# Rounding and widening steps moved from ScalarE to GpSimd, three more warming products and another place for the second layer's weights

## The chip, the core and the metric

The kernel is one program on one core of one Trainium2 chip. The core has five engines with instruction streams of their own: TensorE (PE in the profile; PEld is its loading of weights), VectorE (DVE), ScalarE (ACT), GpSimd (POOL) and SyncE (SP), which here issues all DMA transfers. An engine runs its instructions strictly in the order in which they stand, so one that waits holds up all that stand behind it. The metric is the device time of one execution in microseconds (us), lower is better. TensorE's clock has two levels, 1.2 and 2.4 GHz; the profile gives the granted one as a share of full speed (1.0 or 0.5).

## What is computed

```python
# attention: 4 x 8 heads, 576 positions, head dimension 64
scores = q @ k.T / 8
cum  = cumsum(max(s, 0))
bias = min(-(cum[i] - cum[j]), 0);  causal mask
attn = softmax(scores + bias) @ v
x = attn heads side by side                       # 4 x 576 x 512
# gated part
gate = sigmoid(causal 5-tap convolution of x)     # one filter per channel
x = ((gate * (x @ w_val)) @ w_out)
# mixing part
u = x + (U V along the positions) applied to x    # rank 32
out = u + max(u @ w_ch1, 0) @ w_ch2               # 512 -> 2048 -> 512
```

The weights come in as float64 (the program reads their 32-bit words), q, k, v and s as float32; the result is float32.

## The kernel before

**Products in split form.** Most matrix products are done with operands in the format float32r, each operand cut into a rounded part and a rest: `a = ah + al`, `b = bh + bl`, and `a b` is taken as `ah bh + al bh + ah bl`, so three products for one. Two helpers make the parts: `rnd(kind, o, i)` writes the rounded part, `rest(kind, o, i, hi)` what is left. The name `kind` is looked up in the table `PLAN`, which gives the engine that does the step and a priority (`ahead`; a larger one is put earlier).

**q and k.** Heads 0 to 7, 16 and 30 use q and k as they are. For each of the 22 others `load_raw` brings q and k (transposed, 128 x 576 together) into a tile `qk`, of which there are two; `prep_head` rounds it into `hi` (kind `qk_hi`, line 334), takes the rest into `Q2` (kind `qk_lo`, line 335), and five DMA transfers ("put") lay the halves into the tiles `Q1`, `K1`, `Q2`, `K2` that the score products read. The rows of the profile call these tiles `Q` and `K`.

**Widening.** The weights are float64. `widen` makes the two float32r parts from the words in steps: `wd_a` scales the upper words (line 374), `wd_lim` clamps (line 375, GpSimd), four steps on VectorE (`wd`) build the upper part in `scr` and the lower part in a second scratch tile, and three GpSimd steps write the parts (`wd_hi`, `wd_rest`, `wd_lo`). For the weights of the gate, the value and the mixing products and of the first two blocks of the hidden layer, raw words and scratch lie in pieces of `uT` that are not yet in use (20 runs of `widen`, one of them for the 5 taps, spread between the heads by `side_step`). For blocks 2 to 15 of the hidden layer, raw words come into `raw` tiles and scratch is `scr0` (two buffers) and `scr1` (one), two runs for each block (`widen_w`), 28 in all.

**Attention.** For each head the scores of five blocks of rows are made on TensorE (`sc`), VectorE adds the mask and finds the maximum (`P`), ScalarE takes the exponent (`P`), TensorE turns the result over (`pt`), ScalarE and VectorE copy it out (`PTA`, `PTB`), and for each pair of heads `av` is made from it. Then `norm_rows` and `norm` divide by the row sums (`rs`, `wrs`), do the five taps and the gate. The dense products of a finished batch (`d`) run between the heads of the next.

**Hidden layer.** Sixteen blocks `m` of 128 hidden columns in groups of 2, 2, 3, 4, 3 and 2; for each group all five token tiles `t` are gone through: `ch1` makes 12 products `d` from weights `w1h`, `w1l` and the tokens `u`, ScalarE takes the relu (`hh`), VectorE its rest (`hl`), and `ch2` makes 12 products `acc` from `w2h`, `w2l`. The weights of block `m` lie in place `m % 7` of a ring. Places 0 and 1 lie in the pool `w0`, places 2 and 3 in `wb`, places 4, 5 and 6 in `ml`. `w0` is there from the start; `wb` is opened once the value products of the last batch are recorded, in the memory next to `wa`, which holds `scr0`, `scr1`, `hh` and `hl`; `ml` is opened last, on the other side of the memory, where `wo`, `U4`, `V4` and the gated values of the gated part lie until its last product.

**Order.** The program is recorded as written and then put in order by a scheduler that plays it through with times of its own and takes, for each engine, the ready instruction of the highest priority. So a change of engine or priority moves other instructions too.

**Start.** `WARM` products of 128 x 512 in bf16 on a tile of zeros run before the first scores (line 249).

Of the kernel before, what the change touches and what calls it, by code (L numbers as in the profile page):

```python
# [12 lines left out]
F32R = mybir.dt.float32r  # L13
# [8 lines left out]

PLAN = {
    "pace": ("gpsimd", 0),
    "qk_hi": ("scalar", 6000),
    "qk_lo": ("gpsimd", 2000),
    "put": ("sync", 3000),
    "wd_rest": ("gpsimd", 100),
# [4 lines left out]
    "uh": ("gpsimd", -2000),  # L33
    "ul": ("gpsimd", -6000),
    "u4": ("vector", 0),
    "wd_a": ("scalar", 6000),
    "wd_lim": ("gpsimd", 0),
    "wd": ("vector", -2000),
    "wd_hi": ("gpsimd", -2000),
# [42 lines left out]
RING = 7  # L82
# [7 lines left out]
ORDER = "T0 T1 S0 T2 T3 S1 S2 S3 T4 S4 A0 A1"  # L90
NPD = 6
DT = {"exp": 0.51, "xh": 0.96, "xl": 0.25, "tap": 1.5, "taps": 0.9, "tanh": 1.83, "gv": 4.3, "nl": 3.6, "rows": 10.0, "prep": 1.51}
WARM = 10


@with_exitstack
def fused_kernel(ctx, tc, qT, kT, vP, s, wval, wout, convw, U, V, w1, w2, rows01, out):
    nc = tc.nc
    B, H, D, S = qT.shape
    P = 128  # L100
# [113 lines left out]
    w0 = ctx.enter_context(tc.tile_pool(name="w0", bufs=1, side="right", reuse_waits="tile"))  # L214
# [32 lines left out]
    idle = psV.tile([P, 1024], F32, tag="av", name="idle")[:, 0:512]  # L247
    for _ in range(WARM):
        nc.tensor.matmul(idle, warm[:, 0:P], warm, start=True, stop=True)
# [118 lines left out]
    def widen(raw, scr, hi=None, lo=None, whole=None):  # L368

        a, t = scr  # L370
        au, tu = a.bitcast(U32), t.bitcast(U32)
        shrink = 2.0 ** -112
        steps = [
            lambda: rnd("wd_a", a, raw[..., 1].bitcast(F32), shrink),
            lambda: Via("wd_lim").tensor_scalar(a, a, LIMIT * shrink, -LIMIT * shrink, op0=ALU.min, op1=ALU.max),
            lambda: Via("wd").tensor_scalar(au, au, 3, None, op0=ALU.logical_shift_left),
            lambda: Via("wd").scalar_tensor_tensor(
                au, raw[..., 1], 0x80000000, au, op0=ALU.bitwise_and, op1=ALU.bitwise_or,
            ),
            lambda: Via("wd").tensor_scalar(tu, au, 0xFF800000, None, op0=ALU.bitwise_and),  # L380
            lambda: Via("wd").scalar_tensor_tensor(t, raw[..., 0], 2.0 ** -52, t, op0=ALU.mult, op1=ALU.mult),
        ]
        if whole is not None:
            return steps + [lambda: Via("wd").tensor_add(whole, a, t)]
        return steps + [
            lambda: rnd("wd_hi", hi, a),
            lambda: rest("wd_rest", a, a, hi),
            lambda: Via("wd_lo").tensor_add(lo, a, t),
        ]
# [5 lines left out]
    def pairs(t):  # L395
        return t.bitcast(U32).rearrange("p (n two) -> p n two", two=2)
# [58 lines left out]
    w12 = {m: {x: w0.tile([P, 512], F32R, tag=f"{x}{m}", name=x) for x in ("w1h", "w1l", "w2h", "w2l")} for m in range(2)}  # L455
# [306 lines left out]
    for n in range(NH + 1):  # L762
# [15 lines left out]
        m = n - 1  # L778
# [54 lines left out]
    TW = 512  # L833
# [5 lines left out]
    def load_w(k):  # L839

        m = k // 2
        if m < NF:
            raws[k] = wb.tile([P, 2 * TW], F32, tag="raw", name="raw") if k % 2 else raw1
            nc.sync.dma_start(raws[k].bitcast(U32), words(w2)[m * P:(m + 1) * P, :] if k % 2 else words(w1)[m])

    def widen_w(m):
        pool = w0 if m % RING < 2 else wb if m % RING < 4 else ml
        d = w12[m] = {x: pool.tile([P, TW], F32R, tag=f"{x}{m % RING}", name=x) for x in ("w1h", "w1l", "w2h", "w2l")}

        def part(nm, k):  # L850
            scr = [wa.tile([P, TW], F32, tag=f"scr{k}", name=f"scr{k}", bufs=2 - k) for k in range(2)]
            steps = widen(pairs(raws.pop(k)), scr, hi=d[nm + "h"], lo=d[nm + "l"])

            return steps[:6] + [lambda: load_w(k + 2)] + steps[6:]
        return [
            lambda: part("w1", 2 * m), lambda: part("w2", 2 * m + 1),
            lambda: ready.add(m),
        ]
# [65 lines left out]
    def mlp(i):  # L924

        for _ in pieces(i):
            steps[0] += rate.get(i, 0.0)
            side_step(int(steps[0]))
            steps[0] -= int(steps[0])
            yield  # L930
        if i in due:
            side_work.append(lambda m=due[i]: widen_w(m))
# [23 lines left out]
    wb = ctx.enter_context(tc.tile_pool(name="wb", side="right", **reuse))  # L956
# [6 lines left out]
    ml = ctx.enter_context(tc.tile_pool(name="ml", side="left", **reuse))  # L963
# [50 lines left out]
```

## Time and profile before

| | |
|---|---|
| median of 3 runs | 768.6 us (765.54 to 772.45) |
| the profiled execution | 766.13 us |
| its span, first to last instruction | 764.1 us |
| mean granted clock of TensorE | 0.986 |
| busy: PE, DVE, ACT, POOL | 738.7, 462.1, 300.6, 291.8 us |

The rows further down are of the profiled execution. "Idle" in brackets behind an instruction is the time that its engine stood still before it, and the arrow names what ended that. The starts of matrix products are measured, their ends are modelled, so a PE that is "busy" need not be at its pace. In the view of the chain, the work that ended last is followed back from the end of the execution.

### The profile page before, as it was taken

What the parts mean: (1) busy time and instruction counts of PE and PEld (TensorE: products, weight loads), DVE (VectorE), ACT (ScalarE), POOL (GpSimd) and SP (SyncE); (2) the same over time, 40 slices, a digit from 0 to 9 for tenths busy, and PEclk for the clock granted to TensorE, in tenths of its full rate; (3) what the DMA queues carried; (4) which work ended last, traced back from release to release, by engine and by line L of the source; (5) the groups of instructions that cost most, each with busy time, mean ns of one, the idle gap of its engine ahead of it and who ended that gap; (6) DMA issues with size and microseconds to landing.
All of it is one profiled execution on the core that took longest, in us unless ns stands there. A gap on an engine that the chain in (4) does not pass through costs nothing.

```text
span 764.1 us, 12182 instructions
## 1 busy us (share of the span) xinstructions
PE 738.7 (97%) x4366; PEld 619.2 (81%) x4366; DVE 462.1 (60%) x1053; ACT 300.6 (39%) x788; POOL 291.8 (38%) x323
## 2 busy tenths in 40 slices
PE   8998999999999999999899999999999999999997
PEld 5666889788787998798788888888888888888886
DVE  6878886787558655766749996424582234223234
ACT  5778666875677677533212211111121011010110
POOL 2566566445423243557197765102540024000000
PEclk8989999999999999999999999999999999999999
DMA  4663554644455432021103221100120000000023
GB/s 117 192 182 107 138 128 118 167 126 131 117 125 146 114 97 53 19 82 57 55 1 111 84 97 47 50 0 28 57 84 0 1 28 0 1 1 1 0 111 138
DMA packets 27000, 59.39 MB, mean 78 GB/s; under 512 B 4648, under 2 KB 5288, under 8 KB 26940
## 3 DMA queue, kind: packets, MB, share of 16 engines
q1 hardware_dynamic: 26940, 58.61, 27.2%
q8 instruction: 35, 0.57, 0.3%
q14 instruction: 25, 0.20, 0.1%
HBM read 37.04 MB, written 5.31 MB: 55 GB/s over the span
## 4 chain that ended last, share of the span: by engine, by line
PE 80%; DVE 6%; DMA 5%; ACT 4%; issue 2%; SPq 1%; POOL 1%; ACTq 0%; DVEq 0%; POOLq 0%
PE d L132 37%; PE acc L132 26%; PE pt L132 7%; PE av L132 5%; PE sc L132 5%; DVE uT L132 2%; DMA uT<-in_w 1%; DVE av L614 1%; DMA qk<-in_kT 1%; ACT P L132 1%; DVE P L132 1%; DMA K<-Q 1%; SPq L132 1%; ACT PTA L132 0%; ACT uT L132 0%
## 5 line engine op out<-in xcount | busy, mean ns | idle before, releaser
L132 PE MATMUL d<-u,w1h 128*128 128x512 f32 (+1 forms) x640 | 184.2, 371 | 0.0
L132 DVE SCALAR_TENSOR_TENSOR hl<-d,hh 128x512 fp32r<-128x512 f32 (+1 forms) x80 | 50.7, 634 | 170.4 <-ACT hh L874 170.1
L874 ACT ACTIVATE hh<-d 128x512 fp32r<-128x512 f32 (+1 forms) x80 | 44.3, 555 | 275.2 <-PE acc L132 149.5
L132 PEld LDWEIGHTS d<-u,w1h 128*128 128x128 f32 x640 | 116.0, 188 | 22.2
L132 PE MATMUL d<-u,w1l 128*128 128x512 f32 (+1 forms) x320 | 118.6, 371 | 0.0
L132 PE MATMUL acc<-hl,w2h 128*128 128x512 f32 (+1 forms) x320 | 105.0, 371 | 0.0
L132 PE MATMUL acc<-hh,w2h 128*128 128x512 f32 (+1 forms) x320 | 104.4, 372 | 0.5 <-DVE uT L132 0.5
L132 PE MATMUL acc<-hh,w2l 128*128 128x512 f32 (+1 forms) x320 | 101.9, 371 | 0.0
L132 ACT ACTIVATE P<-P,nm 64x64 f32<-64x64 f32 (+4 forms) x160 | 89.2, 562 | 28.3 <-DVE nm L132 27.9
L132 PE MATMUL sc<-K,Q 68*128 68x288 f32 (+13 forms) x384 | 91.7, 353 | 7.0 <-ACT PTA L132 2.0
L132 PE MATMUL pt<-ident,P 128*128 128x128 f32 x480 | 77.6, 286 | 7.0 <-ACT P L132 3.9
L132 DVE CUSTOM_DVE_ANT_0 P<-sc,causal 64x64 f32<-64x64 f32 (+4 forms) x160 | 65.1, 420 | 31.8 <-PE sc L132 27.6
L132 DVE TENSOR_TENSOR uT<-acc,uT 128x512 f32<-128x512 f32 (+1 forms) x120 | 70.1, 628 | 22.4 <-PE acc L132 22.2
L132 PEld LDWEIGHTS sc<-K,Q 68*128 68x128 f32 (+2 forms) x384 | 64.1, 198 | 16.2 <-ACT PTA L132 2.4
L132 PEld LDWEIGHTS d<-u,w1l 128*128 128x128 f32 x320 | 60.2, 188 | 11.0
L132 PEld LDWEIGHTS acc<-hh,w2h 128*128 128x128 f32 x320 | 58.7, 188 | 12.1 <-issue 0.9
L132 PEld LDWEIGHTS pt<-ident,P 128*128 128x128 f32 x480 | 55.5, 145 | 16.0 <-ACT P L132 7.0
L132 PEld LDWEIGHTS acc<-hl,w2h 128*128 128x128 f32 x320 | 58.8, 188 | 11.2
L132 PEld LDWEIGHTS acc<-hh,w2l 128*128 128x128 f32 x320 | 58.6, 188 | 11.3
L614 DVE SCALAR_TENSOR_TENSOR av<-X,cw,av 128x576 f32<-128x576 f32 x64 | 52.1, 814 | 4.4 <-ACT av L132 4.1
L132 DVE SCALAR_TENSOR_TENSOR scr<-raw,scr 128x512 uint32<-128x512 uint32 (+1 forms) x56 | 52.4, 936 | 1.4
L132 DVE TENSOR_SCALAR scr<-scr 128x512 uint32<-128x512 uint32 x56 | 43.4, 775 | 11.7 <-POOL w1l L132 6.3
(124 smaller groups left out, 1264.6 us busy)
## 6 DMA issues: line engine op xcount, KB each, us to landing
raw<-in_w SPq DMA_DIRECT2D x28, 512.0 KB
K<-hi SPq DMA_DIRECT2D x44, 144.0 KB
Q<-hi SPq DMA_DIRECT2D x44, 144.0 KB
V<-in_vP SPq DMA_DIRECT2D x16, 320.0 KB
out<-uT SPq DMA_DIRECT2D x16, 256.0 KB
qk<-in_qT SPq DMA_DIRECT2D x22, 144.0 KB
qk<-in_kT SPq DMA_DIRECT2D x22, 144.0 KB
K<-Q SPq DMA_DIRECT2D x22, 144.0 KB
```

Source lines behind the costliest of these rows:

```text
L132: return f(*args, **kw)
L614: Via("tap").scalar_tensor_tensor(g, X[:, k:k + S], cw[:, p, k:k + 1], g, op0=ALU.mult, op1=ALU.add,)
L874: Via("hh").activation(h_, o, AF.Relu)
```

## The change

Four edits: the rounding of q and k (`qk_hi`) goes from ScalarE to GpSimd, with priority 2000 in place of 6000; the first widening step (`wd_a`) goes from ScalarE to GpSimd, with priority 0 in place of 6000; `WARM` goes from 10 to 13; and of the places 2 to 6 of the ring, `w2h` and `w2l` now lie in `wb` and `w1h` and `w1l` in `ml`. On GpSimd a rounding is one `tensor_scalar` (line 143).

```diff
 PLAN = {
...
-    "qk_hi": ("scalar", 6000),
+    "qk_hi": ("gpsimd", 2000),
...
-    "wd_a": ("scalar", 6000),
+    "wd_a": ("gpsimd", 0),
...
-WARM = 10
+WARM = 13
...
     def widen_w(m):
-        pool = w0 if m % RING < 2 else wb if m % RING < 4 else ml
-        d = w12[m] = {x: pool.tile([P, TW], F32R, tag=f"{x}{m % RING}", name=x) for x in ("w1h", "w1l", "w2h", "w2l")}
+
+        d = w12[m] = {
+            x: (w0 if m % RING < 2 else wb if x[1] == "2" else ml).tile([P, TW], F32R, tag=f"{x}{m % RING}", name=x)
+            for x in ("w1h", "w1l", "w2h", "w2l")
+        }
```

ScalarE around the rounding of head 14 (`hi`), in the attention of the second batch, before:

```order
L132 ACTIVATE PTB_1289<-pt_1314 128x3x128
L132 ACTIVATE av_1210<-X0_94,cw_86 128x576
L132 ACTIVATE gvh_1369<-d_1330 128x288
L132 ACTIVATE PTB_1289<-pt_1346 128x4x128
L132 ACTIVATE hi_1618<-qk_1452 128x576
L132 ACTIVATE PTA_1288<-pt_1363 128x3x128
L132 ACTIVATE P10_88,sums1_97<-P10_88,nm_1101 128x192
L132 ACTIVATE P20_89,sums1_97<-P20_89,nm_1101 128x320
L132 ACTIVATE uT_58<-uT_58 128x160
```

The same place of ScalarE after the change (the numbers of the tiles are 3 higher):

```order
L132 ACTIVATE PTB_1292<-pt_1317 128x3x128
L132 ACTIVATE av_1213<-X0_94,cw_86 128x576
L132 ACTIVATE PTB_1292<-pt_1349 128x4x128
L132 ACTIVATE PTA_1291<-pt_1366 128x3x128
L132 ACTIVATE gvh_1372<-d_1333 128x288
L132 ACTIVATE P10_88,sums1_97<-P10_88,nm_1104 128x192
L132 ACTIVATE P20_89,sums1_97<-P20_89,nm_1104 128x320
```

The rounding and the scaling of the raw words (`uT_58<-uT_58 128x160`) no longer stand between the copies out of PSUM and the exponents.

GpSimd at about the same place, before (`xh`, `xl`: parts of a finished pair; `woh`, `wol`: parts of the output weights; line 375 is `wd_lim`):

```order
L375 TENSOR_SCALAR uT_58<-uT_58 128x512
L132 TENSOR_SCALAR woh_66<-uT_58 128x512
L143 TENSOR_SCALAR xh0_1310<-X0_94 128x576
L132 TENSOR_TENSOR uT_58<-uT_58,woh_66 128x512
L132 TENSOR_TENSOR xl0_1311<-X0_94,xh0_1310 128x576
L132 TENSOR_TENSOR wol_67<-uT_58 128x512
L132 TENSOR_TENSOR Q2_1455<-qk_1280,hi_1457 128x576
L375 TENSOR_SCALAR uT_58<-uT_58 128x160
```

And after:

```order
L143 TENSOR_SCALAR uT_58<-uT_58 128x512
L375 TENSOR_SCALAR uT_58<-uT_58 128x512
L143 TENSOR_SCALAR xh0_1313<-X0_94 128x576
L132 TENSOR_TENSOR xl0_1314<-X0_94,xh0_1313 128x576
L132 TENSOR_SCALAR woh_66<-uT_58 128x512
L132 TENSOR_SCALAR hi_1621<-qk_1455 128x576
L132 TENSOR_TENSOR uT_58<-uT_58,woh_66 128x512
L132 TENSOR_TENSOR Q2_1458<-qk_1283,hi_1460 128x576
L132 TENSOR_TENSOR wol_67<-uT_58 128x512
L143 TENSOR_SCALAR uT_58<-uT_58 128x160
```

The scaling now stands straight ahead of the clamp, and the rounding of head 14 stands ahead of the rest of head 13 (`Q2_1458`) and of the output weights' parts.

GpSimd at the opening of the hidden layer, before (`u27` is the last part of token tile 2; 5039 to 5042 are the parts of block 2, 5123 of block 3; token tiles 3 and 4 come behind these rows):

```order
L132 TENSOR_TENSOR u27_4872<-uT_58,u26_4871 128x512
L132 TENSOR_TENSOR scr0_5043<-scr0_5043,w1h_5039 128x512
L375 TENSOR_SCALAR scr0_5076<-scr0_5076 128x512
L132 TENSOR_TENSOR w1l_5040<-scr0_5043,scr1_5044 128x512
L132 TENSOR_SCALAR w2h_5041<-scr0_5076 128x512
L375 TENSOR_SCALAR scr0_5127<-scr0_5127 128x512
L132 TENSOR_TENSOR scr0_5076<-scr0_5076,w2h_5041 128x512
L132 TENSOR_TENSOR w2l_5042<-scr0_5076,scr1_5077 128x512
L132 TENSOR_SCALAR w1h_5123<-scr0_5127 128x512
```

And after, where the parts of token tiles 3 and 4 (`u37`, `u47` are their last) stand ahead (5042 to 5045 are the parts of block 2, 5126 and 5127 of block 3):

```order
L132 TENSOR_TENSOR u37_4996<-uT_58,u36_4995 128x512
L132 TENSOR_TENSOR u47_5102<-uT_58,u46_5101 128x256
L132 TENSOR_TENSOR w1l_5043<-scr0_5046,scr1_5047 128x512
L143 TENSOR_SCALAR scr0_5130<-raw1_4430 128x512
L132 TENSOR_TENSOR scr0_5079<-scr0_5079,w2h_5044 128x512
L375 TENSOR_SCALAR scr0_5130<-scr0_5130 128x512
L132 TENSOR_TENSOR w2l_5045<-scr0_5079,scr1_5080 128x512
L143 TENSOR_SCALAR scr0_5169<-raw_5115 128x512
L132 TENSOR_SCALAR w1h_5126<-scr0_5130 128x512
L375 TENSOR_SCALAR scr0_5169<-scr0_5169 128x512
L132 TENSOR_TENSOR scr0_5130<-scr0_5130,w1h_5126 128x512
L132 TENSOR_TENSOR w1l_5127<-scr0_5130,scr1_5131 128x512
```

Blocks 2 and 3 are now made behind the tokens, in the turn that blocks 4 and 5 had before.

## Rows read from the trace of the kernel before

**Rows 1.** The page's first part: busy time, share of the span, instructions.

```profile
PE 738.7 (97%) x4366; PEld 619.2 (81%) x4366; DVE 462.1 (60%) x1053; ACT 300.6 (39%) x788; POOL 291.8 (38%) x323
```

**Rows 2.** Stretches: length, busy time and count of PE, PEld, DVE, ACT, POOL; clock, DMA.

```profile
8.10:14.90 6.80, 6.80 (x25) 4.92 (x24) 4.58 (x19) 4.79 (x16) 0.00 (x0) 0.50 0.52 125
35.40:45.60 10.20, 9.66 (x36) 6.42 (x35) 5.78 (x22) 7.46 (x23) 5.10 (x6) 0.50 0.61 169
...
76.40:324.00 247.60, 236.62 (x1831) 206.05 (x1828) 178.79 (x533) 171.13 (x497) 113.72 (x128) 1.00 0.45 114
...
383.00:764.00 381.00, 376.79 (x1816) 313.65 (x1814) 185.24 (x281) 55.22 (x97) 109.37 (x108) 1.00 0.12 42
```

**Rows 3.** The chain that ended last, in time order: start, length, what.

```profile
6.58 4.48 PE sc L132 x12
...
105.90 3.68 DMA qk<-in_kT
...
267.95 3.57 DMA qk<-in_kT
```

**Rows 4.** ScalarE in order of time: instructions that a load had held up.

```profile
109.69 0.68 ACT L132 ACTIVATE hi<-qk 128x576 fp32r<-128x576 f32 x1 [2.47 <-DMA qk<-in_kT]
...
159.34 0.44 ACT L132 ACTIVATE uT<-uT 128x256 f32<-128x256 f32 x1 [1.28 <-DMA uT<-in_w]
...
184.05 0.45 ACT L132 ACTIVATE uT<-uT 128x256 f32<-128x256 f32 x1 [0.82 <-DMA uT<-in_w]
...
193.12 0.43 ACT L132 ACTIVATE uT<-uT 128x256 f32<-128x256 f32 x1 [1.04 <-DMA uT<-in_w]
...
233.04 0.69 ACT L132 ACTIVATE hi<-qk 128x576 fp32r<-128x576 f32 x1 [0.36 <-DMA qk<-in_kT]
...
271.71 0.69 ACT L132 ACTIVATE hi<-qk 128x576 fp32r<-128x576 f32 x1 [1.48 <-DMA qk<-in_kT]
```

**Rows 5.** Fourteen stretches in which ScalarE stood so, summed: length, then busy.

```profile
sum 27.86, PE 25.82 PEld 21.13 DVE 17.30 ACT 9.47 POOL 14.30; mean PE 1.84 PEld 1.51 DVE 1.24 ACT 0.68 POOL 1.02
```

**Rows 6.** Waits up to 330 us: who waited for whom, us, times, longest.

```profile
POOL uT L375 <- ACT uT L132: 33.1, 15, 14.0
...
ACT hi L132 <- DMA qk<-in_kT: 14.4, 12, 2.5
...
ACT uT L132 <- DMA uT<-in_w: 4.0, 4, 1.3
```

**Rows 7.** Groups by shape up to 330 us: count, busy and mean, idle before.

```profile
L132 ACT ACTIVATE hi<-qk 128x576 fp32r<-128x576 f32 x22 | 15.1, 685 | 18.3 <-DMA qk<-in_kT 14.4 <-DMA uT<-in_U 1.3 <-DMA K<-hi 0.9
...
L132 ACT ACTIVATE uT<-uT 128x512 f32<-128x512 f32 x8 | 5.4, 672 | 1.4 <-POOL wol L132 0.6 <-POOL wvl L132 0.6
```

**Rows 8.** One tile's instructions: count, shortest, median, longest ns, first and last start.

```profile
L132 DVE TENSOR_SCALAR scr<-scr x56: 408/468/1524, 333.9 to 646.8; 128x512 uint32<-128x512 uint32 x56
```

**Rows 9.** TensorE at the start, in order of time.

```profile
1.52 3.87 PE L249 MATMUL idle<-causal 128*128 128x512 bf16 x10 [1.52 <-DVE causal L245]
```

**Rows 10.** The chain in the hidden layer: runs of products.

```profile
434.60 5.69 PE acc L132 x25
...
493.11 8.40 PE acc L132 x36
```

**Rows 11.** GpSimd at the opening of the hidden layer, in order of time.

```profile
381.38 2.11 POOL L132 TENSOR_SCALAR u<-uT 128x512 fp32r<-128x512 f32 x4 [13.81 <-DVE uT L713]
383.45 0.64 POOL L132 TENSOR_SCALAR w1h<-scr 128x512 fp32r<-128x512 f32 x1
...
395.57 1.33 POOL L132 TENSOR_TENSOR w1l<-scr,scr 128x512 fp32r<-128x512 f32 x1
...
406.94 1.36 POOL L132 TENSOR_TENSOR w1l<-scr,scr 128x512 fp32r<-128x512 f32 x1
```

**Rows 12.** TensorE where blocks 2 and 3 begin, in order of time.

```profile
401.56 0.62 PE L132 MATMUL d<-u,w1h 128*128 128x512 f32 x2
...
409.32 0.62 PE L132 MATMUL d<-u,w1h 128*128 128x512 f32 x2
```

## The prediction

> **What bounds the kernel now.** I read the busy times first. PE is at 97% [rows 1], but its ends are modelled, so that figure can't tell work from waiting; the stretches by count can. In the hidden layer, from 383 us on, PE gets through 1816 products in 381 us, nearly all of 512 columns, with no idle time to speak of, while ScalarE is busy 55 us and GpSimd 109 us of it [rows 2]. There only a shorter product or a PE that starves would change the time. In the attention, from 76 to 324 us, no engine is full: DVE 179, ACT 171, POOL 114 of 248 us, and PE's 237 is stretched by products that wait for their inputs [rows 2]. That stretch is a mesh of short waits between four engines that each run in order, and a gain or a loss must come from there or from the start.
>
> Third, the chain of waits, since it says which waits reach the end. Between 100 and 275 us it passes six times through a transfer whose receiver is a ScalarE instruction that the change moves: the first and the last are shown, 3.68 us for q and k of head 14 and 3.57 us for head 31 [rows 3]. ScalarE in order of time then shows how long it stood still at those six: 2.47, 1.28, 0.82, 1.04, 0.36 and 1.48 us [rows 4], each time with a copy out of PSUM or an exponent queued behind.
>
> **What the change does to ScalarE.** It takes 22 roundings of 685 ns, 15.1 us, out of the attention, and the scalings of the raw words: 8 of 672 ns, 5.4 us, and 12 smaller ones that I count as 5 us [rows 7]. So about 25 us of work leave ScalarE there, of 171, and with them the stalls: 14.4 us at the roundings and 4.0 us at the scalings [rows 6]. Of that only what the chain needed counts. The six stalls sum to 2.47 + 1.28 + 0.82 + 1.04 + 0.36 + 1.48 = 7.45 us. I take **7.5 us saved**. The low end comes from fourteen such stretches taken together, 27.86 us long, in which PE was busy 25.82 [rows 5]: PE stood idle only 2.04 us there. The high end is the chain's whole share, six transfers of some 3.6 us, 21 us; I stay near the stalls, because most of each transfer had run before ScalarE reached its place. The 28 scalings in the hidden layer I count at nothing: ScalarE is busy 55 of 381 us there [rows 2], and behind PE's queue nothing waits for it.
>
> **What it does to GpSimd.** The same 25 us of work arrive there, since both engines need about 0.7 us for such a tile; busy time in the attention goes from 114 to about 138 of 248 us, 46 to 56%. Part of it falls into waits that vanish: GpSimd stood 33.1 us before the clamps for ScalarE's scaling, of which 14.0 us were one wait at the start [rows 6], and now it does the scaling itself. What is queued behind a rounding or scaling that waits for its load is the next clamp, the parts `xh` and `xl`, the rest `Q2` and, once per pair, the spreading of the row sums `wrs`. Only `wrs` leads straight to a product. With 10% more of the time taken, 16 times `wrs` meet a 0.7 us instruction in one case of ten and wait half of it, 0.6 us in all; and the stalls of 14.4 + 4.0 us, moved here, are met in 18.4 / 248 = 7% of the cases with about 1 us, 1.2 us in all. **1.8 us lost**, between 0 and the case of the second rival. The rest of a head often stands behind the next head's rounding now, as the order shows; the rest is wanted only a head later, so I count nothing for it, and the same rival is its bound.
>
> **Contention.** VectorE's widening step `scr<-scr`, from SBUF to SBUF, takes 408 ns at best, 468 at the median and 1524 at worst [rows 8]; over the 56 of them, the 19 with no GpSimd instruction beside them have a mean of 418 ns, the 11 with one beside them all the time 1340 ns. In the attention 40 such steps run, of 512 columns or fewer; with GpSimd busy 10% more of the time they lose 40 x 0.1 x (1.5 - 0.4) = 4.4 us of VectorE time at most. VectorE is busy 72% there and its share of the chain is small, so I take **0.6 us lost**, between 0 and 4.4. In the hidden layer VectorE has slack. The Trainium skill (GPSIMD Engine Reference, 1. Specifications) says that GpSimd's SBUF interface is shared with VectorE and contends with VectorE instructions in a two-port mode or with two SBUF inputs, which speaks against putting more on GpSimd. By that rule, taken at the high end, the sum would be 3.8 us worse; the spread of that one instruction agrees with the rule, and the exponents' and maxima's steps that read PSUM are not touched by it.
>
> **Thirteen warming products.** Ten run from 1.52 to 5.39 us [rows 9]; three more, 0.39 us each by the mean of the ten, end by 6.56 us, and the first scores begin at 6.58 [rows 3], so they fit into PE's idle gap and cost nothing. What they can give: behind that gap the clock stood at 0.5, 1.2 GHz, from 8.10 to 14.90 [rows 2]. The scores from 6.58 last 4.48 us, 3 us of them at the low level; at 2.4 GHz these take half, 1.5 us less. Behind them the chain goes over transfers for head 2. I take **0.7 us saved**, the middle of 0 and 1.5.
>
> **The place of the second layer's weights.** The products `acc` of blocks 2 and 3, whose weights lie in `wb`, run 25 in 5.69 us, 228 ns each; those of blocks 4 to 6, from `ml`, 36 in 8.40 us, 233 ns [rows 10]. The change puts the weights of blocks 4, 5, 6, 11, 12 and 13 into `wb`: 6 x 48 full products x 5.7 ns = 1.6 us. In return `w1` of blocks 2, 3, 9 and 10 leaves `wb`; if that costs the same per product for half of the tokens, 4 x 24 x 5.7 ns = 0.5 us. **1.1 us saved**, between 0 and 1.6.
>
> **Blocks 2 and 3.** Their `w1` now lies where the gated part's operands are read until its end, so it can be written no earlier than token tiles 3 and 4, at 381.4 us. Blocks 4 and 5 had that turn before: `w1l` done at 396.9 and 408.3 us [rows 11]. PE wants block 2 at 401.56 and block 3 at 409.32 [rows 12]. So they have a slack of 4.7 and 1.0 us; the added scaling of 0.7 us on GpSimd is made good by its no longer waiting for ScalarE. **Nothing lost**, but up to 5 us if GpSimd slips by one run of `widen` (396.9 to 408.3 is two).
>
> **The sum.** -7.5 + 1.8 + 0.6 - 0.7 - 1.1 = -6.9 us. The profiled execution took 766.13 us, 2 us outside its span, and lies 2.5 us under the median of 768.6; a change in microseconds carries over, so the median becomes 761.7. **Forecast 761.5 us**, 0.9% under before.
>
> **Rivals.** *The stalls were cover for others.* VectorE is busier than ScalarE in the attention (179 to 171 us), and PE was idle only 2.04 us in the fourteen stretches [rows 2, 5]; then the gain is 2.0, less 2.4 lost, with 1.8 from start and place: 767 us. For it speaks that small idle time; against it, that the chain ran through six of them.
>
> *GpSimd becomes the engine that is late.* The place is the pair's end: `wrs` behind a rounding that waits for its load. If each of the 16 pairs meets one stall of 14.4 / 12 = 1.2 us, that is 19 us, and the time 761.5 + 19 - 1.8 = 779 us, slower than before. It decides from 0.5 us per pair on, where 16 x 0.5 eats the gain. For it: GpSimd's order now has roundings and scalings between all its other steps; against: it had 46% load and long waits of its own.
>
> *Blocks 2 and 3 come late*: 761.5 + 5 = 766.5 us; for it speak the 1.0 us of slack and VectorE's four steps between GpSimd's, against it that ScalarE no longer stands in that row.
>
> *The clock.* From 35.4 to 45.6 us it was at 1.2 GHz [rows 2]. If PE, better fed, keeps 2.4 GHz there, half of the 9.66 us of PE time goes: 756.7 us; a new drop of that length elsewhere would cost as much.
>
> *The change doesn't do what it says*: the order shows roundings and scalings on GpSimd, so this is left to the clock at the start, which is in the range.
>
> **How the numbers follow.** Forecast and its neighbourhood (757 to 765) 0.38; a gain above it, by clock or by the high end of the stalls, 0.22; stalls as cover or late blocks, 765 to 771, 0.25; GpSimd late 0.15. A change of 1% (7.7 us) is about what a measurement of this kernel can tell from none; the bound lies at 760.9, inside the forecast's neighbourhood, so 0.20 of its 0.38 is beyond it. Faster by over 1%: 0.22 + 0.20 = 0.42; within 1%: the other 0.18 and the 0.25 of 765 to 771, 0.43; slower by over 1%: 0.15, as GpSimd late mostly means over 776. The range, 749 to 773, leaves out the far end of both sides.
>
> **What will show it.** No ScalarE wait on the loads of q, k or weights; GpSimd with such waits instead, and `wrs` waiting no longer than now. The chain in the attention with fewer transfers. `acc` of blocks 4 to 6 at 228 ns. PE without a wait at blocks 2 and 3. Clock at 1.0 behind 8 us. I would be wrong if PE's waits for `wrs` or for the rests grow, or if the new order lets PE fall idle where it did not.

## The result

The changed kernel took 759.64 us (median of 4 runs, 757.32 to 760.29) beside 767.22 us for the kernel before: a ratio of 0.9898, 95% interval 0.9859 to 0.9938. In a second comparison, with the experiments, it took 756.09 us (4 runs, 754.84 to 756.33) against 765.68 us (18 runs): 0.9865, 0.9839 to 0.9890. The forecast was 761.5 us, 0.9% under before. So the sum came out nearly right; what it was made of came out only in part.

The busy times of the changed kernel answer to [rows 1]. ScalarE lost 36 us, GpSimd gained 46, VectorE 11, and TensorE's (PE's) busy time fell by 5.5 us.

```profile
PE 733.2 (97%) x4369; PEld 617.8 (82%) x4369; DVE 473.0 (62%) x1053; ACT 264.5 (35%) x718; POOL 337.8 (45%) x393
```

The same view as [rows 2], stretches of the changed kernel:

```profile
8.10:14.90 6.80, 6.39 (x40) 4.56 (x39) 4.73 (x19) 5.43 (x19) 0.00 (x0) 1.00 0.54 129
35.40:45.60 10.20, 7.96 (x50) 4.82 (x49) 7.52 (x21) 4.67 (x15) 8.38 (x10) 0.83 0.67 185
76.40:324.00 247.60, 237.43 (x1821) 209.54 (x1820) 184.68 (x534) 157.69 (x462) 134.19 (x160) 0.99 0.45 112
383.00:757.00 374.00, 371.10 (x1796) 310.30 (x1794) 201.28 (x293) 41.25 (x75) 140.39 (x142) 1.00 0.14 48
```

Behind 8 us the granted clock is 1.0 and PE does 40 products where it did 25; between 35 and 46 us it does 50 instead of 36. But from 76 to 324 us, where the forecast's 7.5 us should have come from, PE does no more products in the same time than before (1821 against 1831). That stretch holds low stretches of the clock that come and go; further down it is read without them.

The first two instruction groups of TensorE, the start that answers to [rows 9]: thirteen warming products take 5.73 us, and the first scores begin at 7.04 us, not 6.58. They are quicker, though: 12 take 3.13 us here and took 4.48 us before [rows 3].

```profile
1.52 5.73 PE L249 MATMUL idle<-causal 128*128 128x512 bf16 x13 [1.52 <-DVE causal L245]
7.04 3.13 PE L132 MATMUL sc<-K,Q 66*128 66x64 f32 x12
```

Waits up to 330 us, the view of [rows 6]: what waited, for whom, us in total, times, longest.

```profile
POOL hi L132 <- DMA qk<-in_kT: 22.0, 11, 8.0
POOL wrs L132 <- DVE rs L132: 15.8, 9, 4.4
POOL uT L143 <- DMA uT<-in_w: 9.2, 6, 2.6
PE pt L132 <- POOL wrs L132: 3.9, 2, 2.1
```

ScalarE no longer waits for a load of q and k or of weights; GpSimd waits longer in its place than ScalarE did (22.0 against 14.4 us, 9.2 against 4.0). PE hardly notices. Two roundings on GpSimd in order of time, the second behind the longest of its waits for q and k:

```profile
254.01 0.68 POOL L132 TENSOR_SCALAR hi<-qk 128x576 fp32r<-128x576 f32 x1 [1.57 <-DMA qk<-in_kT]
...
268.00 0.68 POOL L132 TENSOR_SCALAR hi<-qk 128x576 fp32r<-128x576 f32 x1 [7.97 <-DMA qk<-in_kT]
```

PE's longest wait between 258 and 276 us is 0.03 us. From 20 to 100 us the chain goes over GpSimd at two places, both times over `wrs`. GpSimd's steps before 41 us in order of time, and the products that waited for the last of them:

```profile
38.52 1.27 POOL L132 TENSOR_TENSOR wvl<-uT 128x512 fp32r<-128x512 f32 x1
39.88 0.64 POOL L143 TENSOR_SCALAR uT<-uT 128x512 f32<-128x512 f32 x1
40.48 0.72 POOL L132 TENSOR_SCALAR wrs<-rs 128x640 f32<-128x640 f32 x1
```

```profile
41.26 1.16 PE L132 MATMUL pt<-ident,wrs 128*128 128x128 f32 x5 [2.10 <-POOL wrs L132]
```

A moved scaling (line 143) stands right before `wrs`, and PE stood 2.10 us. The scaling itself is 0.64 us of that, and it had waited for no load. The other wait, 1.82 us at 74 us, stands behind a step that was on GpSimd before too (the rest of the output weights, 1.27 us). So this is near the second rival's mechanism, without the load that it named; PE met it twice, 3.9 us in all, not 16 times.

Contention on VectorE is larger than I took it. One group by shape over the whole span, before and then after: the mean of the same 16 widening steps went from 337 to 600 ns.

```profile
L132 DVE TENSOR_SCALAR uT<-uT 128x256 uint32<-128x256 uint32 x16 | 5.4, 337 | 1.7 <-POOL uT L375 1.6
```

```profile
L132 DVE TENSOR_SCALAR uT<-uT 128x256 uint32<-128x256 uint32 x16 | 9.6, 600 | 3.5 <-POOL uT L375 3.3
```

The mean hides that few steps are hit, and these fully: before, one of the 16 took 1137 ns; after, four took 1414 to 1501 and one 528, and the others stayed at 230 to 300 ns. One of the four and the GpSimd step beside it:

```profile
165.97 1.50 DVE L132 TENSOR_SCALAR uT<-uT 128x256 uint32<-128x256 uint32 x1
```

```profile
165.89 1.43 POOL L132 TENSOR_TENSOR xl<-X,xh 128x576 fp32r<-128x576 f32 x1
```

VectorE's step starts 0.08 us behind GpSimd's and ends 0.15 us after it. The other three, and the one before the change, also start during a GpSimd step of 1.4 us with two operands and end 0.14 to 0.15 us after it.

In the hidden layer, the run of products `acc` that [rows 10] shows at 8.40 us, on the chain of the changed kernel:

```profile
488.49 8.17 PE acc L132 x36
```

8.17 / 36 = 227 ns, 233 before. And blocks 2 and 3, GpSimd's last step on `w1` and PE's first product, answering to [rows 11, 12]:

```profile
390.40 1.29 POOL L132 TENSOR_TENSOR w1l<-scr,scr 128x512 fp32r<-128x512 f32 x1
...
401.99 1.36 POOL L132 TENSOR_TENSOR w1l<-scr,scr 128x512 fp32r<-128x512 f32 x1
```

```profile
396.98 0.63 PE L132 MATMUL d<-u,w1h 128*128 128x512 f32 x2
...
404.79 0.63 PE L132 MATMUL d<-u,w1h 128*128 128x512 f32 x2
```

The slack is 396.98 - 391.69 = 5.3 us and 404.79 - 403.35 = 1.4 us; PE did not wait.

### The profile page after: what moved, and what is told of

It reads as the page before. It is cut to its first block, busy times and chain, and to the rows that moved or that the text cites. A ratio compares the mean times of both kernels' runs of the same rounds, so it can differ in the third digit from the quotient of the medians.

```text
span 757.3 us, 12161 instructions
## 1 busy us (share of the span) xinstructions
PE 733.2 (97%) x4369; PEld 617.8 (82%) x4369; DVE 473.0 (62%) x1053; ACT 264.5 (35%) x718; POOL 337.8 (45%) x393
## 3 DMA queue, kind: packets, MB, share of 16 engines
q1 hardware_dynamic: 26940, 58.61, 27.8%
## 4 chain that ended last, share of the span: by engine, by line
PE 85%; DVE 8%; issue 2%; DMA 2%; ACT 2%; POOL 1%; ACTq 0%; DVEq 0%; POOLq 0%
PE d L132 39%; PE acc L132 26%; PE pt L132 8%; PE av L132 6%; PE sc L132 5%; DVE P L132 2%; DVE uT L132 2%; DVE av L614 2%; DMA uT<-in_w 1%; ACT P L132 0%; DMA K<-Q 0%; DVE nl L132 0%; POOL uT L143 0%; DVE uT L313 0%; ACT PTB L132 0%
## 5 line engine op out<-in xcount | busy, mean ns | idle before, releaser
L877 ACT ACTIVATE hh<-d 128x512 fp32r<-128x512 f32 (+1 forms) x80 | 44.3, 556 | 342.8 <-PE acc L132 173.8
L132 ACT ACTIVATE P<-P,nm 128x576 f32<-128x576 f32 (+4 forms) x160 | 89.1, 560 | 36.9 <-DVE nm L132 36.3
L132 PE MATMUL sc<-K,Q 68*128 68x288 f32 (+13 forms) x384 | 87.8, 343 | 2.3 <-ACT PTA L139 1.5
L132 PE MATMUL pt<-ident,P 128*128 128x128 f32 x480 | 75.6, 282 | 5.0 <-ACT P L132 3.0
L132 PEld LDWEIGHTS acc<-hh,w2h 128*128 128x128 f32 x320 | 58.8, 188 | 11.5 <-issue 0.6
L132 PEld LDWEIGHTS acc<-hl,w2h 128*128 128x128 f32 x320 | 58.9, 188 | 10.9 <-DVE hl L132 0.3
L132 DVE SCALAR_TENSOR_TENSOR scr<-raw,scr 128x512 uint32<-128x512 uint32 (+1 forms) x56 | 55.7, 995 | 1.4
```

The costliest lines, as they stand in the source:

```text
L132: return f(*args, **kw)
L877: Via("hh").activation(h_, o, AF.Relu)
```

## The experiments

Twelve kernels in three groups of four, each group beside the kernel before on one chip. The groups ran on three chips, so across groups only ratios are compared. In short, q is the rounding of q and k on GpSimd, w the first widening step there, n thirteen warming products, p the place of the second layer's weights.

**Each edit alone.**

```diff
-WARM = 10
+WARM = 13
```

> The kernel before with thirteen warming products in place of ten, nothing else. By the forecast's own terms 0.7 us less, a ratio of 0.999. By the rival that came out of the trace of the changed kernel, the start: there the clock stood at 1.0 from 8.10 to 14.90 us and the 1.2 GHz stretch of 35.4 to 45.6 us was 3.4 us long instead of 10.2, and the stretch of 76 to 324 us was no shorter; then most of the gain is the clock's, and this kernel gains about 5 us, a ratio near 0.9935, with the granted clock at 1.0 behind 8 us.

Ratio 1.0013 (0.9986 to 1.0040). The stretch behind 8 us shows the clock up as in the changed kernel, and 38 products instead of 25:

```profile
8.10:14.90 6.80, 5.86 (x38) 4.10 (x37) 4.94 (x19) 5.22 (x19) 0.00 (x0) 1.00 0.52 126
```

Yet nothing is left of it at the end. The theory that the start alone makes the gain falls.

```diff
-    "qk_hi": ("scalar", 6000),
+    "qk_hi": ("gpsimd", 2000),
```

> The kernel before with the rounding of q and k on GpSimd, nothing else. By the forecast's terms it takes three of the six stalls away, 2.47 + 0.36 + 1.48 = 4.3 us, and brings some 1.3 us of GpSimd and contention cost: about 3.0 us less, a ratio of 0.996. By the start theory nothing (0.999 to 1.001), since the waits come back on VectorE and GpSimd; clock at 0.5 behind 8 us as before.

0.9966 (0.9940 to 0.9992), 2.6 us: the forecast's term. But in this kernel ScalarE's wait for raw words rose from 4.0 us to

```profile
ACT uT L132 <- DMA uT<-in_w: 10.1, 6, 3.0
```

```diff
-    "wd_a": ("scalar", 6000),
+    "wd_a": ("gpsimd", 0),
```

> The kernel before with the first widening step on GpSimd, nothing else. By the forecast's terms three stalls go, 1.28 + 0.82 + 1.04 = 3.1 us, against some 1.1 us of cost: about 2.0 us less, a ratio of 0.997. By the start theory nothing (0.999 to 1.001). If GpSimd becomes late, slower: the spreading of the row sums then waits longer than before.

1.0010 (0.9977 to 1.0042): nothing where 2.0 us were expected. ScalarE still waits for q and k, and once for v:

```profile
ACT hi L132 <- DMA qk<-in_kT: 13.8, 9, 2.2
...
ACT hi L132 <- DMA V<-in_vP: 7.7, 1, 7.7
```

```diff
-        pool = w0 if m % RING < 2 else wb if m % RING < 4 else ml
...
+            x: (w0 if m % RING < 2 else wb if x[1] == "2" else ml).tile([P, TW], F32R, tag=f"{x}{m % RING}", name=x)
...
```

> The kernel before with the second-layer weights of places 2 to 6 beside the relu's tiles, nothing else. Both theories: 1.1 us less, a ratio of 0.9986, with the products acc of blocks 4 to 6 at 228 ns in place of 233 and the first half of blocks 2, 3, 9 and 10 at 233 in place of 228. If the later turn of blocks 2 and 3 costs, PE waits at 401 or 409 us and the gain is gone.

0.9969 (0.9943 to 0.9995). The trace shows 1.1 us of it where it was expected: from the first product `acc` to the last, 400.3 us against 401.4 before, and the same run of 36 products on the chain:

```profile
495.44 8.17 PE acc L132 x36
```

The rest of the 2.4 us isn't explained by the edit: in its profiled execution this kernel was no faster than before up to the hidden layer.

**One edit left out.** The four ratios alone add up to 0.9958, so either the first figure was lucky or the edits help each other.

> The changed kernel once more, for a closer figure beside the three that follow. The four edits alone gave 1.0013, 0.9966, 1.0010 and 0.9969, which add up to 0.9958. Theory S, each edit by itself: this comes out near 0.994, the high end of its first interval. Theory I, roundings and scalings only help together, because a load that holds ScalarE up through the one takes its toll through the other (with the roundings alone away, its waits for raw words rose from 4.0 to 10.1 us): this stays near 0.990.

0.9865 (0.9839 to 0.9890), so they help each other: the sum 0.9958 is good to some 0.0056 (the root of the four half intervals squared and added; somewhat more, as the four share the runs of the kernel before), and 0.9865 lies 0.0093 from it. With the first comparison's 0.9898 taken in, weighted by the intervals, the changed kernel is at 0.9875, and what follows for single edits is 0.1% less.

> The changed kernel with the first widening step back on ScalarE. Theory S: leaving out an edit that gave nothing alone changes nothing, the ratio is that of the changed kernel. Theory I: ScalarE waits some 10 us for raw words again and loses most of the pair's gain, 4 us above the changed kernel, 0.995.

0.9939 (0.9916 to 0.9961): w, worth nothing alone, is worth 0.7% on top of the others.

> The changed kernel with ten warming products. Theories S and I: the ratio of the changed kernel, within 0.1%, since thirteen alone gave nothing. If the three products help only where the rest of the start is quicker, the clock stands at 0.5 from 8 to 15 us in all its executions and it is 2 to 5 us above the changed kernel, 0.993 to 0.996.

0.9957 (0.9931 to 0.9982): n, worth nothing alone, is worth 0.9%. Theories S and I both miss here; the rider about the three products holds. The profiled execution, 758.6 us, is the second fastest of twelve (758.4 to 767.2), so its trace doesn't show where these 7 us lie.

> The changed kernel with the second-layer weights where they were. Both theories: 1.1 to 2.4 us above the changed kernel, 0.0015 to 0.003 in the ratio, with the products acc of blocks 4 to 6 at 233 ns.

0.9891 (0.9864 to 0.9918): p is worth 0.26%, about what it gave alone, but good only to some 0.4%. Without it the 36 products on the chain are back at 233 ns:

```profile
484.21 8.40 PE acc L132 x36
```

**The pair, the last edit left out, and spare products against the clock.**

> The kernel before with both ScalarE edits, the roundings of q and k and the first widening step on GpSimd, nothing else. The forecast's terms: 7.5 us saved, 1.8 + 0.6 us lost, 5.1 us less, a ratio of 0.9933. Theory S: the two alone add up, 0.9966 + 0.0010, 0.9976. Theory C, the clock decides: without the three warming products the 1.2 GHz stretch behind 8 us stays, and it comes out with the kernel that lacked only those products, less the place's 0.0015: 0.997, with a mean clock near 0.990.

0.9943 (0.9921 to 0.9965), 4.4 us where the forecast's terms gave 5.1. So the pair's size was right. It is more than the two alone add up to (0.9976), but that sum is itself good only to 0.004, so the difference isn't clear of the noise.

> The changed kernel with the rounding of q and k back on ScalarE. Theory S: 0.34% above the changed kernel, 0.990. Theory I, that both kinds of step have to leave ScalarE: ScalarE waits some 10 us and more for q and k, and most of the gain is gone, 0.996 or above. Theory C: its ratio goes with its clock, about 0.35 us for each 0.001 of the mean clock that it lacks against the changed kernel.

0.9995 (0.9975 to 1.0014): without q nothing of the change is left. On top of the other three q is worth 1.3%, alone it gave 0.34%. Theory S falls. Theory I's ratio holds, but not its reason: ScalarE's wait for q and k was 7.7 us here, not over 10.

The last two kernels issue spare products in more heads:

```diff
     def fill(ps, n):
-        if phase[0] <= 2:
+        if phase[0] <= 7:
```

> The kernel before with the two spare products ahead of each transposition, which its first three heads have, issued for heads 3 to 7 as well: some 36 pairs of 0.23 us, 8.3 us of TensorE work that no result needs, between 31 and 80 us. Theory C: the 1.2 GHz stretches of 35 to 45 us and 73 to 76 us vanish, the mean clock rises by some 0.008, up to 6.8 us are regained against what of the 8.3 us is not in idle gaps; the time falls or stays, 0.994 to 1.000. Without the clock's part (the order alone made the change quicker): 2 to 8 us slower, 1.003 to 1.010.

1.0080 (1.0056 to 1.0104), slower. The spare products, one group by shape from 28 to 85 us (35 pairs), took their time:

```profile
L132 PE MATMUL pt<-causal 128*128 128x256 bf16 x70 | 13.2, 281 | 0.5 <-ACT PTA L139 0.4 <-DVE wrs L132 0.2
```

but the mean clock of the runs stayed at 0.987 (before: 0.986). The low stretch moved, to where PE was again short of work:

```profile
47.00:50.40 3.40, 1.59 (x8) 0.99 (x9) 2.69 (x3) 2.79 (x9) 2.42 (x3) 0.68 0.25 57
74.40:81.20 6.80, 4.74 (x20) 3.97 (x19) 6.37 (x21) 5.88 (x16) 2.10 (x4) 0.59 0.43 124
```

So this run doesn't hold the clock up, and what the clock costs by itself can't be read from it.

> The changed kernel with the same spare products for heads 3 to 7. Theory C: its clock is near 1.0 already, so it gains at most one stretch of 3.4 us, 1.7 us, and pays the same work: 0 to 5 us above the changed kernel, and its distance to the kernel before with spare products is smaller than 9.6 us, about 5. If the order alone made the change quicker, the distance stays near 9.6 us.

0.9893 (0.9872 to 0.9915): 2.1 us above the changed kernel (good to some 2.6), as theory C allowed, but the distance to the filled kernel before grew to 14.2 us. Theory C, in the form that an evened-out clock shrinks the distance to 5 us, isn't borne out; nor is the other, that it stays near 9.6.

**Where in the program.** One place can be found in every trace: the first product `av<-PTB,V` of a pair of heads. Here are such rows, TensorE in order of time (narrow windows cut their runs short): for the kernel before the ones of the first, fourth, tenth, fourteenth and sixteenth pair; for the changed one of the first, fourth and sixteenth; for q alone of the same five; and for the changed one in the second comparison of the fourth, tenth and fourteenth.

```profile
27.25 0.55 PE L132 MATMUL av<-PTB,V 128*64 128x192 f32 x4
...
76.73 0.49 PE L132 MATMUL av<-PTB,V 128*64 128x192 f32 x4
...
206.84 0.55 PE L132 MATMUL av<-PTB,V 128*64 128x192 f32 x4
...
286.04 0.55 PE L132 MATMUL av<-PTB,V 128*64 128x192 f32 x4
...
321.62 0.55 PE L132 MATMUL av<-PTB,V 128*64 128x192 f32 x4
```

```profile
25.77 0.55 PE L132 MATMUL av<-PTB,V 128*64 128x192 f32 x4
...
70.38 0.50 PE L132 MATMUL av<-PTB,V 128*64 128x192 f32 x4
...
316.94 0.55 PE L132 MATMUL av<-PTB,V 128*64 128x192 f32 x4
```

```profile
28.58 0.54 PE L132 MATMUL av<-PTB,V 128*64 128x192 f32 x3
...
72.92 0.50 PE L132 MATMUL av<-PTB,V 128*64 128x192 f32 x4
...
207.12 0.55 PE L132 MATMUL av<-PTB,V 128*64 128x192 f32 x4
...
285.01 0.55 PE L132 MATMUL av<-PTB,V 128*64 128x192 f32 x4
...
320.61 0.38 PE L132 MATMUL av<-PTB,V 128*64 128x192 f32 x2
```

```profile
69.78 0.50 PE L132 MATMUL av<-PTB,V 128*64 128x192 f32 x4
...
198.85 0.55 PE L132 MATMUL av<-PTB,V 128*64 128x192 f32 x4
...
276.68 0.55 PE L132 MATMUL av<-PTB,V 128*64 128x192 f32 x4
```

The differences of such rows, and the time at 1.2 GHz in two of the stretches (added up from the granted clock in windows of about 1.7 us), in us; the fourth column is shown once more in parts:

| kernel | to the first pair | first to fourth | of it at 1.2 GHz | fourth to sixteenth | fourth to tenth | of it at 1.2 GHz | tenth to fourteenth | `acc`, first to last |
|---|---|---|---|---|---|---|---|---|
| before | 27.2 | 49.5 | 14 | 244.9 | 130.1 | 0 | 79.2 | 401.4 |
| p | 27.2 | 49.8 | 17 | 246.9 | 131.2 | 0 | 80.1 | 400.3 |
| n | 26.1 | 49.1 | 11 | 247.8 | 132.7 | 2 | 79.5 | 401.4 |
| w | 27.9 | 50.7 | 19 | 252.2 | 136.9 | 8 | 79.8 | 401.5 |
| n, p, w | 26.0 | 51.3 | 17 | 247.1 | 132.2 | 10 | 79.4 | 400.4 |
| q | 28.6 | 44.3 | 7 | 247.7 | 134.2 | 0 | 77.9 | 401.4 |
| q, n, p | 26.5 | 44.1 | 7 | 248.1 | 134.6 | 0 | 77.8 | 400.4 |
| q, w | 32.0 | 41.7 | 0 | 244.9 | 131.1 | 0 | 78.2 | 401.5 |
| q, w, p | 27.8 | 44.3 | 3 | 242.9 | 129.2 | 7 | 78.1 | 401.1 |
| q, w, n | 26.0 | 42.3 | 0 | 244.3 | 129.5 | 0 | 77.8 | 401.4 |
| all | 25.8 | 44.6 | 3 | 246.6 | 133.2 | 7 | 77.8 | 400.4 |
| all, again | 25.9 | 43.9 | 3 | 244.0 | 129.1 | 0 | 77.8 | 400.4 |

Most columns show one edit. The first falls to about 26 us with n. The second is 49 to 51 us without q and 42 to 45 with it, in every kernel. The fourth is 243 to 247 us with q and w together, 247 to 252 with one of them, 245 to 248 with neither. The last falls by 1 us with p (by 0.3 in q, w, p). Two cautions: the kernel before and p run the same attention and differ by 2 us in the fourth column; and each row is one execution, that of w the slowest of its twelve runs, that of q, w, p the second fastest.

The fourth column mixes in low stretches of the clock; its parts can be read without them. From the fourth to the tenth pair, seven traces have none: the kernel before and p take 130.1 and 131.2 us, the two kernels with q and without w 134.2 and 134.6, the three with both 129.1 to 131.1. So there q alone costs 3 to 4 us, and w takes that back. ScalarE's waits for raw words show how: 4.0 us before, 10.1 with q alone, none with w, and in q, n, p

```profile
ACT uT L132 <- DMA uT<-in_w: 12.9, 6, 3.9
```

The difference between q, n, p and the changed kernel there, 5.5 us, is about what w was worth on top of the others. From the tenth to the fourteenth pair no trace has a low stretch: 79.2 to 80.1 us without q, 77.8 to 78.2 with it, in every kernel.

**The clock.** In q and w together, PE was late between 18 and 29 us, and lost at the start what it won later:

```profile
18.30:28.50 10.20, 8.70 (x30) 5.97 (x32) 6.66 (x27) 6.19 (x19) 4.14 (x7) 0.55 0.53 176
```

The low stretches also change from one execution of a program to the next. Two stretches of the changed kernel, in the first comparison and in the second; the second line of each starts some 12 us behind the first `av<-PTB,V` of the fifteenth pair:

```profile
75.60:79.00 3.40, 3.40 (x17) 3.34 (x16) 2.07 (x9) 2.59 (x8) 1.72 (x3) 0.50 0.71 230
312.40:315.80 3.40, 3.34 (x28) 2.81 (x29) 1.75 (x7) 1.31 (x4) 2.81 (x4) 1.00 0.00 0
```

```profile
75.60:79.00 3.40, 3.40 (x28) 3.37 (x27) 3.36 (x12) 3.33 (x11) 2.59 (x3) 1.00 0.68 176
307.80:311.20 3.40, 3.40 (x17) 2.25 (x18) 0.75 (x3) 1.00 (x3) 2.11 (x3) 0.50 0.00 0
```

From the fifteenth to the sixteenth pair the ten traces of the table without a low stretch there take 16.7 us, and the two with one, of 3.4 us (q, w, n, and all, again), 18.1 and 18.2. So in that place a low stretch cost 1.5 us, 0.44 of its length. Taken at that price (an estimate), the low stretches make up most of the second column's difference: its mean is 50.1 us without q and 43.6 with it, and 43.2 and 42.1 with 0.44 of the low time taken off.

Over the 179 runs of the second comparison and the experiments, each kernel taken against its own level, a run whose mean clock is 0.010 lower takes 3.4 us longer. 0.010 of some 765 us is 15 us at the low level, which would cost 7.6 us if PE were at work all that time; by this slope it costs less than half of that, as it would if PE waited in much of it anyway. The changed kernel's mean clock was 0.998 in the second comparison and that of the kernel before 0.985; 0.013 of clock would be some 4.4 of the 9.6 us by this slope. From kernel to kernel the slope is twice that: over the ten without added spare products the ratios fall by 6.6 us for each 0.010 that the mean clock rises, and by that nearly all of the 9.6 us would go with the clock. Both are correlations, and the one attempt to set the clock failed, so the share is argued, not shown.

## Why the prediction was right, and where not

**ScalarE relieved, 7.5 us saved and 5.1 net.** The size holds: q and w alone measured 4.4 us. The place holds only in small part. I read the gain off six stalls between 100 and 275 us [rows 3, 4]. They are gone, and from 80 to 320 us the chain passes 4 transfers instead of 11. Four of the six, 5.6 us, lie between the fourth and the tenth pair; there the traces without a low stretch take 129.1 to 131.1 us with both edits and took 130.1 and 131.2 before, some 1 us less. There the rival that the stalls were cover for other work was nearly right, as the 2.04 us of idle PE said [rows 5]; and the kernel n, p, w, no quicker than before, has 5 transfers on its chain, so their count is no measure of the gain. The other two stalls, 1.8 us, lie between the tenth and the fourteenth pair, and there every kernel with q is 1.0 to 2.3 us shorter than those without. What I also left out is that q alone moves ScalarE's waits to the raw words; it takes w to undo that. The largest difference lies between the first and the fourth pair, 27 to 77 us: where two kernels differ in q alone it is 5 to 9 us shorter with q. I had not read that stretch: the roundings' waits there are small, and I looked for waits. My first reading was ScalarE's load. From 27 to 77 us it was busy 39.6 of 50 us before and 35.1 after (the fourth engine in these two lines), more densely than in [rows 2] later, and a rounding there stands as work ahead of exponents.

```profile
27.00:77.00 50.00, 44.66 (x274) 32.47 (x274) 40.08 (x118) 39.58 (x113) 30.95 (x32) 0.86 0.55 154
```

```profile
27.00:77.00 50.00, 43.33 (x298) 32.38 (x295) 42.60 (x120) 35.10 (x109) 36.98 (x42) 0.95 0.63 172
```

The first is the kernel before, the second the changed one, with 24 products more. But with w alone ScalarE was busy 36.6 us there, with n, p and w 35.2, and nothing came of it, so load doesn't explain it. What goes with q is the time at 1.2 GHz in this stretch, from 11 to 19 us without it to 7 at most: by the estimate of 0.44 us for each us of it, all but some 1 of the 6.5 us. So the gain there comes mostly with the clock; why the low stretches shrink with q and not with w stays open.

**GpSimd, 1.8 us lost.** It waits for loads longer than ScalarE did, once 8 us, and nothing followed. `wrs` waited 15.8 us for the row sums, 14.2 before. PE's waits for `wrs`, none before, came to 3.9 us: a sign that I had named for being wrong. That is more than I took, and it fell at 41 and 74 us, not spread over the pairs. The load that moves was misread too: I set 25 us, counted up to 330 us, against the 171 of the stretch from 76 to 324 us; there ScalarE lost 13.4 us and GpSimd gained 20.5. The second rival's 0.5 us per pair was not reached.

**Contention, 0.6 us lost.** VectorE's busy time grew by 10.9 us with the same 1053 instructions (7.2 in the second trace); from 76 to 324 us it grew by 5.9 (5.4), more than the 4.4 us I set as the most for the attention. Of the sixteen small widening steps five instead of one were held up. The Trainium skill (GPSIMD Engine Reference, 1. Specifications) speaks of contention on the SBUF interface that GpSimd shares with VectorE, for VectorE instructions in a two-port mode or with two SBUF inputs. These steps, from SBUF to SBUF with one input, agree with it if they ran in that mode, which no row shows. The chain of the changed kernel passes one of them, at 137.72 us with 1.50 us, so 1.2 us of it can lie on the time there; the second trace's chain passes none. The bound was too small; whether the 0.6 us was too, no row shows.

**Thirteen warming products, 0.7 us saved.** The mis-sized term. They do not fit into the gap (first scores 0.46 us later), the clock behind them stays up from 8 to 15 us in five of the table's six traces that have them (with q, n and p it falls for 3.4 us at 11.5), and the first pair comes 1.1 to 2 us earlier in the kernels that differ in n alone (6 us for q and w, in one execution): about my high end. But by the medians n is worth nothing on the kernel before and 0.9%, some 7 us, on top of the other three; on top of q and w it is 0.5% (0.9943 to 0.9891). I had counted "behind that the chain goes over transfers" as the end of the matter. That a shifted start moves everything behind it, the low stretches of the clock with it, is my reading; no trace shows where the 7 us lie.

**The place of the weights, 1.1 us saved.** Right: 401.4 to 400.4 us from the first to the last `acc`, by 227 against 233 ns per product in the place that changed. In the whole time it is at the edge of what can be told.

**Blocks 2 and 3.** Right: slack 5.3 and 1.4 us, against 4.7 and 1.0 worked out.

**The clock as a rival, 756.7 us.** The second comparison's 756.09 us lies there, and the stretch named, 35 to 46 us, did stay at 2.4 GHz for most of its length. It was not a rival to the main forecast but came with the same edits.

So the forecast was right by its sum, and partly by luck. The pair's 5.1 us was right in size and mostly wrong in place, and n was priced alone where its worth depends on the other edits.

## What to carry to other kernels

A stall on the chain need not be worth its length: where PE idled 2 of 28 us, 5.6 us of stalls gave some 1 us. Take for a milestone a product that every version has, and compare the stretches between; it shows within one execution which edit acts where, and comparing only stretches at equal clock keeps the clock's ups and downs out of it. Edits to a program that a scheduler puts in order need not add up: two that gave nothing alone gave 0.7 and 0.9% with the others, one of them because it removes a wait that another edit makes longer. So test what is lost when one is taken away, not only each alone.

## What was not expected of the hardware

The clock's low stretches are not a property of the program alone: the kernel before ran with mean clocks from 0.979 to 0.995 in 71 runs and 762.1 to 772.8 us, and the changed kernel's two traces have them at different places. Some 35 pairs of spare products between 28 and 85 us did not raise the mean clock of the kernel before (0.987 against 0.986) and cost 6.1 us by the ratio. With q alone and ten warming products the clock behind 8 us was at 1.0 in the profiled execution, so that low stretch isn't tied to their number alone. A VectorE step of 0.29 us took 1.50 us when it began just behind a GpSimd step of 1.43 us, and ended with it. And waiting is cheap on an engine that nobody is waiting for: GpSimd stood 8 us for a load at 260 us, and PE's longest wait from 258 to 276 us was 0.03 us.
